# A fused attention and expert kernel: the first expert blocks loaded inside the last attention group

## The chip, the cores and the metric

The kernel runs on one core of a Trainium2 chip. TensorE (PE in the profile) multiplies, VectorE (DVE) and ScalarE (ACT) do elementwise work, GpSimd (POOL) and SyncE (SP) issue DMAs, POOL those that scatter rows by an index. The metric is the device time of one execution in microseconds (us), as the median of several.

## The reference, cut to what matters

There are 8 batches of 2,496 rows. The attention output becomes the expert layer's input, row by row; each token has one expert of eight, given by a hash of its id.

```python
scores = (1.0 / S) * np.matmul(z, z.transpose(0, 2, 1))   # z: (8, 2496, 64)
attn = np.maximum(scores, 0.0) ** 2
x = (u * np.matmul(attn, v)).reshape(B * S, D)             # D = 256
expert_idx = token_ids * np.int64(2654435761) % np.int64(E)   # E = 8
for e in range(E):
    mask = expert_idx == e
    out[mask] = np.maximum(x[mask] @ w1[e], 0.0) @ w2[e]   # w1: 256x1024, w2: 1024x256
```

With the inputs used, the experts have 2,506, 2,446, 2,582, 2,478, 2,498, 2,473, 2,434 and 2,551 tokens.

## The kernel before, in words

The tile framework derives every wait from what an instruction reads and writes; the order of instructions on each engine is the order in which the program issues them (`order = tc.manual_schedule()`, line 439). An instruction that waits holds back all that stands behind it on its engine or queue.

**Attention.** A batch's rows make 20 tiles, 19 of 128 rows and one of 64. Four tiles make a group, so there are 5 groups a batch and 40 in all (line 453), written here as (batch, group), the last (7,4). For each group the loop of lines 475 to 523 runs over the inner tiles t: `attend` (line 253) accumulates attention times v in PSUM, `square` and `turn_scores` prepare squared scores, and `scores` of the next group stand near the group's end. Scores are symmetric: in batches after the first, a block that is already made for one group is turned by DVE into a "mirror" tile (`turn_scores`, line 207) and read from there by a later group. There are six mirror tiles of 128 x 2048 numbers, in a pool that opens with group 4 and closes behind the last group (`mirror_pool`, lines 472, 482 and 527). `attend_short` (line 226) does the short tile of a batch, `gate` and `gate_short` multiply with u and give rows of x on DVE.

**Routing.** `places` (line 297) is a generator whose small steps, one per call of `between` (line 457), are strewn over the first groups: from the token ids it counts tokens by expert (matmuls at line 345, copies at 346, a scan at 350), and works out each token's slot. Slots are ordered by expert, each expert padded to blocks of 256 slots, at most 85 blocks. Steps with a bare `yield` (line 336) are idle. `enter` then writes the token numbers by slot to memory, and the list comes back as `idx` (line 428): the token of each slot, or N for an empty slot. `eb_i` holds each block's expert, `used` the number of blocks in use. `place_x` (line 430) scatters a tile of x rows to their slots in `x_rows` (`x_dram` in the code) by a POOL DMA; it too is called from `between`.

**Experts.** After the last group all remaining `place_x` calls are issued. For each block of 256 slots, `load_w` (line 541) reads the block's expert number into a register on SP and issues five DMAs for the two weight matrices, `load_x` (line 550) issues four for the block's x, `turn_x` (line 558) transposes it on DVE, `up` (line 562) is the first layer with its relu on ACT or DVE, `down` (line 576) the second layer for 128 slots, with a copy on ACT and a scatter to the output by a POOL DMA (rows with an index beyond the output are skipped). `run` (line 588) strings blocks together: `up` of block j runs between the two `down` of block j - 1, and loads run two blocks ahead into three sets of buffers. The weights' buffers are a pool of their own, which lies where the mirror tiles were.

**Tail.** 79 blocks run unconditionally, then a branch on `used` (line 615) covers blocks 81 to 84, which are made if more than 81 are in use, and the last two blocks follow behind it. On an untaken branch each engine jumps over its part and brings the semaphore counts up to date.

Of the kernel before, what the change touches and what calls it, by code (L numbers as in the profile page):

```python
# [10 lines left out]
F32 = mybir.dt.float32  # L11
BF16 = mybir.dt.bfloat16
I32 = mybir.dt.int32
AF = mybir.ActivationFunctionType
OP = mybir.AluOpType
AX = mybir.AxisListType
# [8 lines left out]
def kernel(  # L25
# [10 lines left out]
    nc = tc.nc  # L36

    B, S, D = u.shape
    K = z.shape[-1]
    N = B * S  # L40
    E, _, F = moe_w1.shape
# [3 lines left out]
    P = 128  # L45
    TM = S // P
    SM = TM * P
    R = S - SM
    T = TM + 1
    assert R == 64 and K == 64  # L50
    G = 4
    NG = T // G
# [12 lines left out]
    def pool(name, bufs, **kw):  # L65
        return ctx.enter_context(tc.tile_pool(name=name, bufs=bufs, **kw))
# [81 lines left out]
    def turn_z(b, g):  # L148
        if g == 0:
            zT[b] = zpool.tile([P, T * P], F32, name="zT")  # L150
        o = zT[b][:, ts(g, G * P)]
        if b:
            nc.vector.transpose(o, zn[b][:, ts(g, G)].rearrange("p t j k -> p (t j k)"))
            return
        ps = mm_ps.tile([P, G * P], F32, name="z_ps", tag="mm")
        for i, t in enumerate(group(g)):
            nc.tensor.transpose(ps[:, ts(i, P)], zn[b][:, t].rearrange("p h k -> p (h k)"), ident[:])  # L157
        nc.scalar.copy(o, ps[:])
# [76 lines left out]
    def gate_short(b, ps):  # L235
        nc.scalar.copy(odd[:], ps[R:P, :])  # L236
        x = x_sb[b, NG - 1] = xpool.tile([P, G, D], F32, name="x_sb")
        nc.vector.tensor_add(odd[:], odd[:], ps[0:R, :])  # L238
        nc.vector.scalar_tensor_tensor(out=x[0:R, G - 1, :], in0=odd[:], scalar=c2, in1=u_sb[b, NG - 1][0:R, G - 1, :],
                                       op0=OP.mult, op1=OP.mult)  # L240
        gated.append((b * T + TM, x[0:R, G - 1, :]))
# [11 lines left out]
    def attend(b, g, t, acc, queries):  # L253
        for i in queries:
            if i in whole(g):
                nc.tensor.matmul(acc[i // 2][:, i % 2, :], lhs(b, g, t, i), v_sb[b][:, t, :],  # L256
                                 start=(t == 0 and i % 2 == 0), stop=(t == TM - 1), skip_group_check=True)
# [15 lines left out]
    idx = const.tile([P, NS], I32)  # L273
    eb_i = const.tile([1, NB], I32)
    used = const.tile([1, 1], I32)
    slot_i = const.tile([P, C], I32)
    addr = const.tile([P, C], I32)
    token = const.tile([P, B, T], I32)
# [18 lines left out]
    def places():  # L297

        with tc.tile_pool(name="route", bufs=1) as route:
# [33 lines left out]

            for _ in range(6):
                yield
            total = route.tile([P, E, C], F32)
            rank = route.tile([P, E, C], F32)
            H = 512 // C  # L340
# [40 lines left out]
            nc.vector.tensor_sub(shift[:], ends[:], blocks[:])  # L381
            yield
            nc.vector.scalar_tensor_tensor(shift[:], shift[:], float(BLK), first[:], op0=OP.mult, op1=OP.subtract)
            yield


# [68 lines left out]
    i = 0  # L455
# [13 lines left out]
            place_x()  # L469
        i += 1  # L470

    mirror_pool = ExitStack()
    scores(0, 0)
    square(EARLY)
    for n, (b, g) in enumerate(groups):
        if n + 1 < len(groups):
            load_u(*groups[n + 1])
        if g == 0 and b + 1 < B:
            load_z(b + 1)
            load_v(b + 1)  # L480
        if n == NG - 1:
            m = mirror_pool.enter_context(tc.tile_pool(name="mirror", bufs=1))
            mirrors = [m.tile([P, G, G, P], F32, name=f"m_{k}") for k in range(NG * NG // 4)]

        acc = [acc_ps.tile([P, 2, D], F32, name="acc", tag="acc") for _ in range(2)]
        for k in range(2):
            for t in range(EARLY):
                attend(b, g, t, acc, [2 * k, 2 * k + 1])
            square(2)
            turn_scores(2)  # L490
            between()
        for t in range(EARLY, TM - LATE):
            if g == NG - 1 and b + 1 < B and t % 2 == 0 and t // 2 <= NG:
                turn_z(b + 1, t // 2 - 1)
            attend(b, g, t, acc, range(G))
            if t % G == G - 1 and (b, t // G, g) in mirror and g < NG - 1:
                mirrors.append(mirror.pop((b, t // G, g)))
            square(2)
            turn_scores(2 + (t % 3 == 0))
            between()  # L500
        assert not to_square
        if g == NG - 1:
            gate_short(b, attend_short(b))
            mirrors.extend(mirror.pop(k) for k in sorted(mirror))
        attend_last(b, g, acc)
        between()
        if n + 1 < len(groups):

            while len({k[:3] for k in to_turn}) + len(fresh(*groups[n + 1])) // G > NG + (g + 1 < NG):
                turn_scores(1)  # L510
            scores(*groups[n + 1])
        square(3)
        turn_scores(3)

        for k in range(2):
            for t in range(TM - LATE, TM):
                attend(b, g, t, acc, [2 * k, 2 * k + 1])
            for q in (2 * k, 2 * k + 1):
                gate(b, g, q, acc)
            square(2)  # L520
            turn_scores(2)
            between()
        between()
    assert not to_turn and next(place, None) is None and i > 2 * T + 4 * C
    while gated:
        place_x()
    mirror_pool.close()

    LOADS = 3
    wpool = pool("wpool", 1)
    opool = pool("opool", 4)
    w1_buf = [wpool.tile([P, DP, F], F32, name=f"w1_{k}") for k in range(LOADS)]
    w2_buf = [wpool.tile([P, FP, D], F32, name=f"w2_{k}") for k in range(LOADS)]
    xg_all, xT_all = (zpool.tile([P, T * P], F32, name="zT") for _ in range(2))
    xg_buf = [xg_all[:, ts(k, DP * BLK)].rearrange("p (k d) -> p k d", d=D // NQ) for k in range(LOADS)]
    xT_buf = [xT_all[:, ts(k, DP * BLK)].rearrange("p (k h i) -> p k h i", h=DP, i=Q) for k in range(LOADS)]
    w1, w2, xg, xT, hT = {}, {}, {}, {}, {}

    def load_w(j, k):
        w1[j], w2[j] = w1_buf[k], w2_buf[k]
        e = nc.sync.value_load(eb_i[0:1, j:j + 1], min_val=0, max_val=E - 1)
        for r in range(NQ):
            rows = moe_w1[ds(e, 1), ts(r, D // NQ)].rearrange("one d f -> (one d) f")
            nc.sync.dma_start(w1[j][ts(r, Q)], rows.rearrange("(h i) f -> i h f", i=Q))
        nc.sync.dma_start(
            w2[j][:], moe_w2[ds(e, 1)].rearrange("one f d -> (one f) d").rearrange("(c p) d -> p c d", p=P))

    def load_x(j, k):  # L550

        xg[j] = xg_buf[k]
        for r in range(NQ):
            nc.sync.dma_start(
                xg[j][ts(r, Q)],
                x_dram[ts(j, BLK), ts(r, D // NQ)].rearrange("(k i) d -> i k d", i=Q))

    def turn_x(j, k):
        xT[j] = xT_buf[k]
        nc.vector.transpose(xT[j].rearrange("p k h i -> p (k h i)"), xg[j].rearrange("p k d -> p (k d)"))  # L560

    def up(j, f):
        ps = mm_ps.tile([P, 2, BLK], F32, name="h_ps", tag="mm")
# [9 lines left out]
        else:  # L573
            nc.vector.tensor_scalar_max(o, ps[:], 0.0)  # L574

    def down(j, t):
        ps = acc_ps.tile([P, D], F32, name="o_ps", tag="acc")
        for f in range(FP):
            nc.tensor.matmul(ps[:], hT[j][:, f, ts(t, P)], w2[j][:, f, :], start=(f == 0), stop=(f == FP - 1))  # L579
        o = opool.tile([P, D], F32, name="o_sb")  # L580
        nc.scalar.copy(o[:], ps[:])  # L581
        st = nc.gpsimd.indirect_dma_start(  # L582
            out=out[:], out_offset=bass.IndirectOffsetOnAxis(ap=idx[:, j * TB + t:j * TB + t + 1], axis=0),
            in_=o[:], in_offset=None, bounds_check=N - 1, oob_is_err=False)
        tc.declare_no_dep(st.ins, group="rows", reason="each token has its own row")
        tc.add_to_no_dep_group("rows", st.ins)

    def run(first, last, loads):

        for j in range(first, last + 1):  # L590
            if j < last and j + 2 < loads:
                load_x(j + 2, (j + 2) % LOADS)
            for f in range(0, FP, 2):
                if j < last:
                    up(j, f)
                if j > first and f % 4 == 2:
                    down(j - 1, f // 4)
                if f == 2 and j < last and j + 1 < max(last, loads):
                    turn_x(j + 1, (j + 1) % LOADS)
            if j < last and j + 2 < loads:  # L600
                load_w(j + 2, (j + 2) % LOADS)
# [3 lines left out]

    NU = -(-N // BLK) + E // 2 - 1
    NM = NU - 2
    for j in range(2):
        load_w(j, j)
    for j in range(2):  # L610
        load_x(j, j)
    turn_x(0, 0)
    run(0, NM, NU)
    n_used = nc.values_load(used[0:1, 0:1], min_val=1, max_val=NB)
    with tc.If(n_used > NU):
        for j in range(NU, NB):
            load_x(j, (NM + 2) % LOADS)
            load_w(j, (NM + 2) % LOADS)
            turn_x(j, (NM + 2) % LOADS)
            run(j, j + 1, 0)  # L620
    run(NM, NU, 0)

    order.__exit__(None, None, None)
# [28 lines left out]
```

## Time and profile before

| | us |
|---|---|
| median of 3 runs | 2717.02 (2716.9 to 2718.02) |
| profiled execution, its own time | 2718.32 |
| its span in the profile | 2716.4 |
| PE busy | 2681.2 (99%) |
| DVE busy | 1190.3 (44%) |
| ACT busy | 576.2 (21%) |
| POOL busy | 478.7 (18%) |
| expert matmuls, both layers (L566, L579) | 587.2 + 585.2 |

Times in the trace count from the span's start. PE is the matmul row, PEld its weight loads, which overlap. Matmuls on 32-bit numbers appear as two records each. "L566" is line 566 of the kernel before. A bracket at a line's end tells how long the engine stood idle before it and what released it. Names of DMA queues end in q (SPq, POOLq). Buffers that share a pool's tag appear by the tag's name: x of a block and its transpose are both zT, the weights w. Attention ends and the expert layer begins at about 1572 us; the branch of the tail lies at about 2681 us.

### The profile page before, as it was taken

Reading aid. Unit: us, or ns where it says so; the run is one execution under the profiler, and the core shown is the slowest. Engines: PE = TensorE matmul, PEld = TensorE weight load, DVE = VectorE, ACT = ScalarE, POOL = GpSimd, SP = SyncE. Lnnn points to the kernel's source line nnn. Section 1 sums busy time; section 2 is a strip of 40 time slices with the busy share of each in tenths; the row PEclk is TensorE's granted clock in tenths of the full one; section 3 lists DMA queues with packets and bytes.
Section 4 is the critical chain, followed back from the end, with each engine's and each line's share of the span. In section 5 each row is a group of like instructions: output and inputs, shape, how many; then the busy total and the mean of one; then the engine's idle time right before and its main releaser. Section 6 shows DMA issues by size and latency. Waiting matters only on the chain.

```text
span 2716.4 us, 32950 instructions
## 1 busy us (share of the span) xinstructions
PE 2681.2 (99%) x12650; PEld 2250.2 (83%) x12650; DVE 1190.3 (44%) x1875; ACT 576.2 (21%) x1151; POOL 478.7 (18%) x500
## 2 busy tenths in 40 slices
PE   8999999999999999999999979999999999999998
PEld 6777887888888887887878868888888888888887
DVE  5655956848838838758659411111111111111111
ACT  2013214214222233123132101111111111111111
POOL 0221222122212221222101111111111111111111
PEclk9999999999999999999999989999999999999999
DMA  9612113013103121031101077777777777777773
GB/s 283 212 31 73 32 31 88 16 32 88 31 23 82 31 50 60 26 89 32 32 15 31 23 191 189 188 188 188 194 190 193 191 189 191 190 189 188 189 186 104
DMA packets 334256, 308.84 MB, mean 114 GB/s; under 512 B 186732, under 2 KB 293117, under 8 KB 334096
## 3 DMA queue, kind: packets, MB, share of 16 engines
q1 hardware_dynamic: 309424, 264.78, 38.5%
q0 software_dynamic: 20496, 41.10, 5.0%
q8 instruction: 102, 1.67, 0.3%
q10 hardware_dynamic: 4176, 0.82, 0.2%
q14 instruction: 58, 0.48, 0.1%
HBM read 243.25 MB, written 64.13 MB: 113 GB/s over the span
## 4 chain that ended last, share of the span: by engine, by line
PE 55%; issue 37%; POOL 6%; DMA 2%; POOLq 0%; DVE 0%
PE acc L256 44%; PE s_ps L181 8%; POOL out_dram L582 5%; PE acc L250 1%; DMA out_dram<-o_sb,idx 1%; PE q_ps L231 1%; DMA zn<-in_z_dram 0%; POOLq L582 0%; POOL x_rows L433 0%; PE z_ps L157 0%; DVE upto L350 0%; DVE x_sb L265 0%; DVE a L202 0%; POOLq L647 0%; PE cnt_ps L345 0%
## 5 line engine op out<-in xcount | busy, mean ns | idle before, releaser
L256 PE MATMUL acc<-v_sb,a 128*128 128x256 f32 x3760 | 826.8, 380 | 2.5 <-DVE a L202 1.4
L256 PEld LDWEIGHTS acc<-v_sb,a 128*128 128x128 f32 x3760 | 711.0, 190 | 128.0 <-issue 29.0
L215 DVE STREAM_TRANSPOSE m<-a 32x512 f32<-32x512 f32 (+1 forms) x1120 | 757.2, 676 | 19.5 <-ACT a L200 2.7
L566 PE MATMUL h_ps<-zT,w 128*128 128x256 f32 x2592 | 587.2, 380 | 16.5 <-DMA zT<-x_rows 15.3
L579 PE MATMUL o_ps<-w,hT 128*128 128x256 f32 x2592 | 585.2, 379 | 0.0
L566 PEld LDWEIGHTS h_ps<-zT,w 128*128 128x128 f32 x2592 | 493.6, 191 | 84.6 <-issue 15.7
L579 PEld LDWEIGHTS o_ps<-w,hT 128*128 128x128 f32 x2592 | 492.5, 190 | 66.9
L574 DVE TENSOR_SCALAR hT<-h_ps 128x512 f32<-128x512 f32 x162 | 112.0, 691 | 951.4 <-PE h_ps L566 951.4
L256 PE MATMUL acc<-v_sb,m 128*128 128x256 f32 x2016 | 439.7, 379 | 0.0
L256 PEld LDWEIGHTS acc<-v_sb,m 128*128 128x128 f32 x2016 | 383.1, 190 | 52.0
L188 ACT ACTIVATE a<-s_ps 128x512 f32<-128x512 f32 (+1 forms) x365 | 193.6, 593 | 913.5 <-PE s_ps L181 905.0
L433 POOL DMA_INDIRECT x_rows<-x_sb,slot_i x160 | 157.8, 986 | 1089.8 <-DVE x_sb L265 917.1
L582 POOL DMA_INDIRECT out_dram<-o_sb,idx x162 | 157.5, 972 | 978.8 <-ACT o_sb L581 964.0
L181 PE MATMUL s_ps<-zT 64*128 64x512 f32 (+1 forms) x1040 | 230.4, 586 | 0.0
L186 DVE TENSOR_SCALAR a<-s_ps 128x512 f32<-128x512 f32 (+1 forms) x155 | 106.0, 684 | 283.1 <-PE s_ps L181 282.0
L200 ACT ACTIVATE a<-a 128x512 f32<-128x512 f32 (+1 forms) x420 | 221.5, 623 | 0.0
L581 ACT COPY o_sb<-o_ps 128x256 f32<-128x256 f32 x162 | 60.3, 372 | 743.7 <-PE o_ps L579 743.7
L181 PEld LDWEIGHTS s_ps<-zT 64*128 64x128 f32 x1040 | 116.8, 187 | 89.1 <-issue 61.5
L421 POOL DMA_INDIRECT slot_tokens<-token,addr x160 | 159.3, 996 | 161.2 <-DVE addr L415 110.9
L572 ACT ACTIVATE hT<-h_ps 128x512 f32<-128x512 f32 x162 | 96.7, 597 | 242.1 <-PE h_ps L566 242.1
L265 DVE SCALAR_TENSOR_TENSOR x_sb<-acc,u_sb 128x256 f32<-128x256 f32 x152 | 57.7, 419 | 58.4 <-PE acc L256 57.8
L238 DVE TENSOR_TENSOR odd<-odd,q_ps 64x256 f32<-64x256 f32 x8 | 3.3, 414 | 168.9 <-ACT odd L236 168.9
(67 smaller groups left out, 331.5 us busy)
## 6 DMA issues: line engine op xcount, KB each, us to landing
w<-in_moe_w_dram SPq DMA_DIRECT2D x324, 256.0 KB, 6.7
w<-in_moe_w_dram SPq DMA_DIRECT2D x81, 1024.0 KB, 6.1
x_rows<-zero SPq DMA_DIRECT2D x10, 2176.0 KB, 15.0
zT<-x_rows SPq DMA_DIRECT2D x324, 64.0 KB, 6.0
v_sb<-in_v_dram SPq DMA_DIRECT2D x32, 512.0 KB, 4.5
u_sb<-in_u_dram SPq DMA_DIRECT2D x32, 512.0 KB, 4.0
zn<-in_z_dram SPq DMA_DIRECT2D x28, 304.0 KB, 5.6
v_sb<-in_v_dram SPq DMA_DIRECT2D x8, 384.0 KB, 7.3
```

The costliest lines, as they stand in the source:

```text
L181: nc.tensor.matmul(ps[:, 0:n], zT[b][h, ts(t, P)], zT[b][h, ds(g * G * P, n)], start=True, stop=True)
L186: nc.vector.tensor_scalar_max(a, ps[:, 0:n], 0.0)
L188: nc.scalar.activation(a, ps[:, 0:n], AF.Relu)
L200: nc.scalar.square(o, x)
L215: nc.vector.transpose(mirror[b, a, g][ts(c, Q)].rearrange(squares)[:, 0:m, ts(r, Q)], made[b, a, g][ts(r, Q)].rearrange("p t (s q) -> p (t ...
L256: nc.tensor.matmul(acc[i // 2][:, i % 2, :], lhs(b, g, t, i), v_sb[b][:, t, :], start=(t == 0 and i % 2 == 0), stop=(t == TM - 1), skip_gr ...
L421: st = nc.gpsimd.indirect_dma_start(out=slot_dram[:, None], out_offset=bass.IndirectOffsetOnAxis(ap=addr[0:n, c:c + 1], axis=0), in_=token ...
L433: st = nc.gpsimd.indirect_dma_start(out=x_dram[:, :], out_offset=bass.IndirectOffsetOnAxis(ap=slot_i[0:width(c % T), c:c + 1], axis=0), in ...
L566: nc.tensor.matmul(ps[:, i, :], w1[j][:, c, ts(f + i, P)], xT[j][:, :, c, :], start=(c == 0), stop=(c == DP - 1))
L574: nc.vector.tensor_scalar_max(o, ps[:], 0.0)
L579: nc.tensor.matmul(ps[:], hT[j][:, f, ts(t, P)], w2[j][:, f, :], start=(f == 0), stop=(f == FP - 1))
L582: st = nc.gpsimd.indirect_dma_start(out=out[:], out_offset=bass.IndirectOffsetOnAxis(ap=idx[:, j * TB + t:j * TB + t + 1], axis=0), in_=o[ ...
```

## The change

In the last group, (7,4), and without a branch, the program now issues: the weights of block 0 at inner tile 5, the x of blocks 0 and 1 at inner tile 10, the turns of both at inner tiles 14 and 15, and the weights of block 1 after the short tile. The weights' buffers are the six mirror tiles themselves: the two that are free in the last group for block 0, the four that it reads for blocks 1 and 2. The pool of mirrors no longer closes, and the weights' own pool is gone.

At inner tile 10 the rows of group (7,4) are not yet in `x_rows`. Tokens are numbered so that late tokens have the last places within their expert; `places` works out, per expert, the slot of the first late token (`late`), the least of these (`least`), and whether it lies within the first two blocks: `redo` is N (19,968) then and 0 otherwise, `good` is N if it does not and 0 otherwise. These are five new steps of `places`, and five of the six idle ones are gone. `extra` is `used` plus `redo` and takes its place in the branch. If the branch is taken, it now also makes blocks 0 and 1 again, besides 81 to 84.

The output scatters of the branch move behind it: its results go to `o_all`, a tile of 128 x 5120 numbers that POOL clears before block 0, and twelve scatters from there follow the branch on POOL in any case. Two small DVE maxima make `once` and `again`, the index lists of blocks 0 and 1 for their first and second making; of the two, only the first writes rows when `redo` is 0. POOL takes no part in the branch any more; PE, ACT, DVE and SP do.

```diff
@@ places
-            for _ in range(6):
-                yield
+            yield
...
+            late = route.tile([P, E], F32)
+            nc.vector.tensor_add(late[:], shift[:], upto[:, :, C - G - 1])
+            yield
+            least = route.tile([P, 1], F32)
+            nc.vector.tensor_reduce(least[:], late[:], axis=AX.X, op=OP.min)
+            yield
+            for o, op in ((redo, OP.is_lt), (good, OP.is_ge)):
+                nc.vector.tensor_scalar(o[:], least[:], float(AHEAD * BLK), float(N), op0=op, op1=OP.mult)
+                yield
+            nc.vector.tensor_add(extra[:], used[:], redo[0:1, :])
+            yield
@@ the loop over groups
-            m = mirror_pool.enter_context(tc.tile_pool(name="mirror", bufs=1))
+            m = pool("mirror", 1)
...
+            if n + 1 == len(groups) and t == T // 4:
+                w_buf = list(mirrors)
+                w_buf.extend(mirror[b, a, g] for a in range(NG - 1))
+                load_w(0, 0)
+            if n + 1 == len(groups) and t == T // 2:
+                assert not gated
+                xg_all, xT_all = (zpool.tile([P, T * P], F32, name="zT") for _ in range(2))
...
+                for k in range(AHEAD):
+                    load_x(k, k)
+            if n + 1 == len(groups) and t >= TM - LATE - AHEAD:
+                turn_x(t - (TM - LATE - AHEAD), t - (TM - LATE - AHEAD))
...
             gate_short(b, attend_short(b))
+            if n + 1 == len(groups):
+                load_w(1, 1)
@@ before the expert blocks
-    wpool = pool("wpool", 1)
+    o_all = vpool.tile([P, T, D], F32, name="v_sb")
+    nc.gpsimd.memset(o_all[:], 0.0)
+
+    once = const.tile([P, AHEAD * TB], I32)
+    again = const.tile([P, AHEAD * TB], I32)
+    for o, x in ((once, redo), (again, good)):
+        nc.vector.tensor_tensor(o[:], idx[:, 0:AHEAD * TB], x[:].to_broadcast([P, AHEAD * TB]), op=OP.max)
@@ down
-        o = opool.tile([P, D], F32, name="o_sb")
+        k = j * TB + t
+        if later is not None:
+            o = o_all[:, len(later), :]
+            later.append((o, again[:, k:k + 1] if j < AHEAD else idx[:, k:k + 1]))
+        else:
+            o = opool.tile([P, D], F32, name="o_sb")
         nc.scalar.copy(o[:], ps[:])
+        if later is None:
+            store(o[:], once[:, k:k + 1] if j < AHEAD else idx[:, k:k + 1])
@@ the tail
-    for j in range(2):
-        load_w(j, j)
-    for j in range(2):
-        load_x(j, j)
-    turn_x(0, 0)
     run(0, NM, NU)
-    n_used = nc.values_load(used[0:1, 0:1], min_val=1, max_val=NB)
+    n_used = nc.values_load(extra[0:1, 0:1], min_val=1, max_val=NB + N, engines=[
+        mybir.EngineType.PE, mybir.EngineType.Activation, mybir.EngineType.DVE, mybir.EngineType.SP])
+    later = []
     with tc.If(n_used > NU):
-        for j in range(NU, NB):
+        for j in [*range(AHEAD), *range(NU, NB)]:
             load_x(j, (NM + 2) % LOADS)
             load_w(j, (NM + 2) % LOADS)
             turn_x(j, (NM + 2) % LOADS)
-            run(j, j + 1, 0)
+            run(j, j + 1, 0, later)
+    for o, rows in later:
+        store(o, rows)
     run(NM, NU, 0)
```

## The prediction

> **What bounds the kernel now.** I began with the page. TensorE (PE) is busy 99% of the span, so a time can change only where PE stands still, runs at a lower clock, or gets other work. PE's work is the same matmuls before and after. The second part of the page, 40 slices of 67.9 us, shows one hole, the "7" in the 24th slice (1562 to 1630 us), and the granted clock lower in the same slice. The group of the first expert layer names its cause: x, 15.3 us.
>
> ```profile
> PE   8999999999999999999999979999999999999998
> PEclk9999999999999999999999989999999999999999
> ...
> L566 PE MATMUL h_ps<-zT,w 128*128 128x256 f32 x2592 | 587.2, 380 | 16.5 <-DMA zT<-x_rows 15.3
> ```
>
> Next the list of waits, where PE's own lines are few; the third is in the first batch:
>
> ```profile
> PE h_ps L566 <- DMA zT<-x_rows: 15.3, 1, 15.3
> ...
> PE h_ps L566 <- ACTq L615: 1.2, 1, 1.2
> ...
> PE acc L256 <- DVE x_sb L265: 1.1, 1, 1.1
> ```
>
> Then the timeline at 1563 to 1588 us. The last attention matmul (L256, from 1571.65, 0.38 us) ends at 1572.03. The last rows of x leave POOL at 1574.04, SP can ask for x only when they have landed, at 1581.61, DVE turns block 0 at 1586.52, and PE starts at 1587.33. The weights of blocks 0 and 1 (4 MB) go out only from 1566.18, after the last reader of the mirror tiles, and share the DMA engines with those last rows.
>
> ```profile
> 1566.18 1.93 SPq L546 DMA_DIRECT2D w<-in_moe_w_dram  x4
> ...
> 1574.04 0.97 POOL L433 DMA_INDIRECT x_rows<-x_sb,slot_i  x1 [0.31 <-issue]
> 1581.61 5.76 SPq L554 DMA_DIRECT2D zT<-x_rows  x12
> 1586.52 0.71 DVE L560 STREAM_TRANSPOSE zT<-zT 128x512 f32<-128x512 f32 x1 [14.02 <-DMA zT<-x_rows]
> ...
> 1587.33 12.36 PE L566 MATMUL h_ps<-zT,w 128*128 128x256 f32 x48 [15.30 <-DMA zT<-x_rows]
> ```
>
> Last the same place by windows (columns: window, its us, busy of PE, PEld, DVE, ACT, POOL, then granted clock, DMA share, GB/s). After the hole PE runs at half clock until about 1591.
>
> ```profile
> 1572.00:1587.30 15.30, 0.03 (x1) 0.00 (x0) 1.14 (x2) 0.00 (x0) 2.40 (x3) 0.67 1.02 273
> 1587.30:1589.10 1.80, 1.77 (x4) 1.51 (x5) 0.00 (x0) 0.00 (x0) 0.00 (x0) 0.50 0.40 92
> 1589.10:1591.00 1.90, 1.90 (x6) 1.47 (x5) 0.00 (x0) 0.00 (x0) 0.00 (x0) 0.53 0.86 235
> 1591.00:1593.00 2.00, 2.00 (x11) 1.77 (x10) 0.18 (x1) 0.60 (x1) 0.00 (x0) 1.00 1.01 207
> ```
>
> **Change, 1: block 0 is ready before attention ends.** Weights 0 go to two mirror tiles last read in group (7,3) at inner tiles 4 to 11, about 1509.5 to 1526.8; SP has been idle since 1507.8 (it stood 57.0 us in front of the weight loads, by its own waits). Five DMAs issue in 2.5 us and land in 6.7: in place by about 1536. The eight x DMAs wait for the four scatters of group (7,3), the last of which issues at 1543.72; with a landing of 2.4 us (8.4 at most in this stretch) they issue from 1547.1 (1553) for 8 x 0.48 = 3.8 us and land 6.0 us later: 1557 (1563). DVE turns two blocks, 2 x 0.7 us, done by 1558.5 (1564.5). Behind these turns on DVE stands the short tile's add at 1567.37, and behind the x loads on POOL the short tile's scatter at 1568.51: both later than the later value. So PE can go on at 1572.03: **-15.30 us**.
>
> **2: the clock.** 48 matmul records after the hole take 12.36 us; 48 in the tail take 10.52 (2670.06). Without the hole that is **-1.84 us** (half clock over 3.9 us would say 1.95; I take the records). Here a rule is to be weighed: the tail's 1.2 us stall leaves the clock at 1.00, the 15.3 us hole does not. The Trainium skill (TensorE: Matmul & The Clock Gate, Part 1: The HAM clock gate) puts the limit at an idle window of about 3.4 us. By the rows alone, any remaining stall over 1.2 us might keep the 1.84 us; by the rule only one over 3.4. For the main sum both say the same, as no stall remains; for the rivals I use the rule.
>
> **3: blocks 1 and 2 in time?** Block 0 has no second-layer work of a predecessor, so it lasts 32 records, 6.9 us: block 1 is due at 1578.9, block 2 (13.8 later) at 1592.8. Weights 1 wait for the first two mirrors of group (7,4) to be read by the short pass (L231 from 1562.36, 0.46 us per four matmuls): issue about 1563.5 to 1566.3, landed 1573: 6 us early. Block 2's x waits for the last scatter (1574.04, landing 2.4 to 8.4 us): 1576.4 to 1582.4, plus 2 us of issue and 6 us: 1584.5 to 1590.5. Its first-layer weights issue behind it on SP: 2.5 us and 6.7 us more: landed 1588 to 1594. Taken: 1588, since only 2 MB instead of 4 compete with the scatters. Cost 0; at the far end 1.2 us. DVE waits for this x with only a relu behind it that is due at 1589. From block 3 on the SP order is the old one.
>
> **4: the new steps on POOL and DVE before block 0.** POOL clears a 128x5120 tile: the 128x1280 memset took 1.16 us, so an estimated 4.6 us, from 1575.0 to 1579.6, ahead of the first result store at about 1588. The Trainium skill (SBUF — State Buffer, SBUF: two separate sides) speaks against it: GpSimd and some VectorE forms share a port pair by exclusive lock. No run here shows the two together. By the trace the two small maxima (128x4, nearest row 0.16 us) cost 0.3 us of DVE; by the rule they might wait 4.6 us. The first relu behind them is needed at 1582.4 (first second-layer matmul), so by either the sum is 0; without that cover it is at most 4.6.
>
> **5: the routing steps five slots earlier.** Five idle slots go, five small DVE operations (0.15 us each, DVE has gaps there) come later, so the number of slots stays. The count matmuls move to after 7 inner tiles instead of 12: 24.17 + 56 records x 0.2187 = 36.4 us, and the mask they need is done at 32.58. DVE's two last pairs of squares now wait for counts, until 38.9 and 40.9; PE needs the first of them at 52.9 (the short tile, L250). Scan and rank sums (5.8 us) run in the gap at 46.8 to 52.8, before the next relu at 55.45. What it gives: in group 1 the 2.82 us scan stood between two gates and made PE wait.
>
> ```profile
> 67.80 2.82 DVE L350 TENSOR_TENSOR_SCAN upto<-ones,total 128x1280 f32<-128x1280 f32 x1
> 70.53 0.73 DVE L265 SCALAR_TENSOR_TENSOR x_sb<-acc,u_sb 128x256 f32<-128x256 f32 x2
> ...
> 71.32 26.17 PE L256 MATMUL acc<-v_sb,a 128*128 128x256 f32 x120 [1.11 <-DVE x_sb L265]
> ```
>
> The scan's place is taken by a 0.16 us operation: **-1.11 us**.
>
> **6: the tail.** Expert 0 has 2,506 tokens in slots 0 to 2,505, and the late 448 tokens of 19,968 are some 50 of them, so the first late slot is near 2,455, not below 512: the branch stays untaken and blocks 0 and 1 stand. PE's stall of 1.2 us there follows ACT's count at 2681.7, behind its copy, and stays (0). PE's own branch took 3.94 us on its sequencer (2677.2 to 2681.2, the branch line's rows), mostly behind queued matmuls; it now jumps over six block bodies instead of four. One row can't tell whether that matters: taken 0, and if it grew with the bodies, to 5.9 us, PE would start 1.9 later. New are twelve stores on POOL between branch and last two blocks, every row out of range. The trace has one such store: expert 2 has 2,582 tokens, so tile 1 of its last block is empty, the 62nd store:
>
> ```profile
> 2025.18 0.97 POOL L582 DMA_INDIRECT out_dram<-o_sb,idx  x1 [5.93 <-ACT o_sb L581]
> ...
> 2681.31 0.97 POOL L582 DMA_INDIRECT out_dram<-o_sb,idx  x1 [2.48 <-ACT o_sb L581]
> 2696.59 0.97 POOL L582 DMA_INDIRECT out_dram<-o_sb,idx  x1 [14.31 <-ACT o_sb L581]
> ...
> 2710.36 0.97 POOL L582 DMA_INDIRECT out_dram<-o_sb,idx  x1 [2.48 <-ACT o_sb L581]
> ```
>
> It costs no more than the others. Back to back POOL takes 1.28 us a scatter (1572.76 to 1574.04): 12 x 1.28 = 15.4 us, from 2682.6 to 2698.0 in the old times. The store due at 2696.59 is 1.4 us late, the next (2703.50) on time, the end not moved. They become path once each takes more than (2710.36 - 3 x 1.28 - 2682.6)/12 = 2.0 us.
>
> **Sum.** 15.30 + 1.84 + 1.11 = 18.25. Profiled span 2716.40 - 18.25 = 2698.15; the profiled run's own 2718.32 gives 2700.07; it was 1.30 above the median of the runs, 2717.02, which gives **2698.8**.
>
> **Rivals.** (B) *Block 1 or 2 starves.* For it: DMA is at its share of 1.0 around the hole. Against: half the bytes compete. A stall of 1 to 4 us, with the clock's 1.84 above 3.4: 2700 to 2704.6. (C) *The tail turns slower.* The twelve stores serialise on their landings: 12 x 5.4 us (the median of these stores) = 64.8, from 2682.6 to 2747.4; the last store then goes at 2751.2 instead of 2710.36, 40.9 later: 2739.7. It decides from 2.0 us a store, and eats the gain at 3.5. Against: the wait of a store is for the one eight before it, 10 us back. (D) *The early loads do not come early*, because the x loads wait for the last scatters after all: only step 5 and part of the weights' crowding are won, about 2712 to 2716. Against: the scatters of the last group come later in the program than the loads.
>
> **How the numbers follow.** A 0.80 (own range 2697.3 to 2700.7, with the jump's 1.9), B 0.11, D 0.04, C 0.05. A change within 0.2%, 5.4 us, can hardly be told from none here; and D lies there. Faster 0.91, same 0.04, slower 0.05. For 8 in 10 the range takes A and B: 2697.0 to 2704.0.
>
> **What would show it.** PE's wait for zT gone from the waits, clock 1.00 at 1570 to 1592, x loads issued near 1547, no PE wait on x_sb near 71, twelve stores 1.28 us apart with no longer last gap. Wrong, if PE waits for weights or x in blocks 1 or 2, or if the last store comes late behind the twelve.

## The result, and the profile after

| | before | after |
|---|---|---|
| median of the runs, us | 2717.52 (4 runs, 2716.9 to 2718.03) | 2699.97 (4 runs, 2699.02 to 2701.16) |
| profiled execution, its own time | 2718.32 | 2699.9 |
| span | 2716.4 | 2698.2 |

The ratio of the runs is 0.9933, with a 95% interval of 0.9921 to 0.9945: 17.6 us faster, against 18.25 forecast; the range held. The span, 2698.2, was forecast as 2698.15.

The second part of the page of the changed kernel, and the group of the first expert layer (its line is now L600): the hole and the dip of the clock are gone, and of that group's 16.5 us of waiting 1.2 are left.

```profile
PE   8999999999999999999999999999999999999998
PEclk9999999999999999999999999999999999999999
...
L600 PE MATMUL h_ps<-zT,m 128*128 128x256 f32 x2592 | 585.3, 379 | 1.2 <-ACTq L655 1.2
```

All of PE's waits that its list has are these; x_sb in the first batch is gone too, and what is left was there before:

```profile
PE z_ps L157 <- DMA zn<-in_z_dram: 9.2, 1, 9.2
...
PE acc L256 <- DVE a L202: 1.4, 1, 1.4
PE h_ps L600 <- ACTq L655: 1.2, 1, 1.2
```

The timeline at the seam. SP asks for x of blocks 0 and 1 at 1544.57, 25 us before PE needs it; DVE turns both by 1552.2; PE's last attention group runs into the first expert matmuls with nothing between (1566.00 + 4.15 = 1570.15; ends of matmuls are modelled and overlap a little). Block 2's x and weights follow at 1574.57 and 1577.21.

```profile
1544.57 3.79 SPq L496 DMA_DIRECT2D zT<-x_rows  x8
1548.37 0.71 DVE L512 STREAM_TRANSPOSE zT<-zT 128x512 f32<-128x512 f32 x1 [7.75 <-DMA zT<-x_rows]
1551.48 0.71 DVE L512 STREAM_TRANSPOSE zT<-zT 128x512 f32<-128x512 f32 x1 [2.41 <-DMA zT<-x_rows]
...
1561.60 1.87 SPq L506 DMA_DIRECT2D m<-in_moe_w_dram  x4
...
1566.00 4.15 PE L256 MATMUL acc<-v_sb,a 128*128 128x256 f32 x18
1569.99 10.52 PE L600 MATMUL h_ps<-zT,m 128*128 128x256 f32 x48
...
1573.17 4.37 POOL L589 MEMSET v_sb<- 128x5120 f32 x1
1573.64 0.69 DVE L608 TENSOR_SCALAR hT<-h_ps 128x512 f32<-128x512 f32 x1 [2.88 <-PE h_ps L600]
1574.57 1.79 SPq L496 DMA_DIRECT2D zT<-x_rows  x4
```

And the tail, with the first and the last of the twelve new stores (of v_sb), and the first and the last of the four stores that follow them:

```profile
2662.62 10.63 PE L600 MATMUL h_ps<-zT,m 128*128 128x256 f32 x48 [1.22 <-ACTq L655]
2663.41 0.98 POOL L625 DMA_INDIRECT out_dram<-v_sb,again  x1 [0.30 <-issue]
...
2677.49 0.98 POOL L625 DMA_INDIRECT out_dram<-v_sb,idx  x1 [0.30 <-issue]
...
2678.78 0.98 POOL L625 DMA_INDIRECT out_dram<-o_sb,idx  x1 [0.30 <-issue]
...
2691.19 0.97 POOL L625 DMA_INDIRECT out_dram<-o_sb,idx  x1 [2.48 <-ACT o_sb L620]
```

**Where the 18.2 us of the span went.** The wait for the first z, and four distances between marks, in both traces:

| stretch | before | after | difference |
|---|---|---|---|
| start to the first matmul (wait for z) | 9.46 | 9.15 | -0.31 |
| first matmul to the end of attention | 1562.57 | 1561.00 | -1.57 |
| end of attention to the first second-layer matmul | 1572.03 to 1599.53: 27.50 | 1570.15 to 1580.35: 10.20 | -17.30 |
| that matmul to the start of the last store | 1110.83 | 1110.84 | 0.0 |
| start of the last store to the end | 6.05 | 7.01 | +0.96 |

The sum is -18.2. The first difference is chance (the z wait of other runs lies between 9.2 and 9.5 us); the next three are the steps of the prediction; the last is a cost that it did not have.

### The profile page after: what moved, and what is told of

Read it like the earlier page. It is cut to its first block, busy times and chain, and to the rows that moved or that the text cites. A ratio compares the mean times of both kernels' runs of the same rounds, so it can differ in the third digit from the quotient of the medians.

```text
span 2698.2 us, 32995 instructions
## 1 busy us (share of the span) xinstructions
PE 2678.7 (99%) x12650; PEld 2248.9 (83%) x12650; DVE 1191.3 (44%) x1882; ACT 576.4 (21%) x1151; POOL 495.8 (18%) x513
## 5 line engine op out<-in xcount | busy, mean ns | idle before, releaser
L600 PE MATMUL h_ps<-zT,m 128*128 128x256 f32 x2592 | 585.3, 379 | 1.2 <-ACTq L655 1.2
L613 PE MATMUL o_ps<-m,hT 128*128 128x256 f32 x2592 | 585.2, 379 | 0.0
L600 PEld LDWEIGHTS h_ps<-zT,m 128*128 128x128 f32 x2592 | 492.4, 190 | 68.5 <-ACTq L655 1.6
L613 PEld LDWEIGHTS o_ps<-m,hT 128*128 128x128 f32 x2592 | 492.5, 190 | 67.0
L181 PE MATMUL s_ps<-zT 64*128 64x512 f32 (+1 forms) x1040 | 230.4, 586 | 0.0
L181 PEld LDWEIGHTS s_ps<-zT 64*128 64x128 f32 x1040 | 116.9, 187 | 89.1 <-issue 61.5
```

Of the source, the lines that this page charges most:

```text
L181: nc.tensor.matmul(ps[:, 0:n], zT[b][h, ts(t, P)], zT[b][h, ds(g * G * P, n)], start=True, stop=True)
L600: nc.tensor.matmul(ps[:, i, :], w1[j][:, c, ts(f + i, P)], xT[j][:, :, c, :], start=(c == 0), stop=(c == DP - 1))
```

## The experiments

All times are medians; "changed" is the changed kernel, 2699.97, or 2699.79 (5 runs) where it ran again on the chip of the experiment, as here:

> The changed kernel once more, to stand beside the next three on one chip: 2700.0, and from the last packet of the last store to the end of POOL's drain 3.9 us, against 2.9 in the kernel before.

Measured: 2699.79 (2699.35 to 2700.74), ratio 0.9932 (0.9919 to 0.9946). In its trace the last packet of the last store ends 4.98 us ahead of the span's end, where the kernel before has 4.03 (both to the span's end, where the expectation counts to the drain's, so each is some 1.1 above the expectation's figures): the 0.96 us shows again.

### The x loads late, the weights early

```diff
-                for k in range(AHEAD):
-                    load_x(k, k)
-            if n + 1 == len(groups) and t >= TM - LATE - AHEAD:
-                turn_x(t - (TM - LATE - AHEAD), t - (TM - LATE - AHEAD))
...
     while gated:
         place_x()
+    for k in range(AHEAD):
+        load_x(k, k)
+    for k in range(AHEAD):
+        turn_x(k, k)
```

> The changed kernel, with only the x loads and turns of blocks 0 and 1 put back behind the last scatters; the weights of block 0 stay early. Theory (the hole is the chain scatter, landing, x load, turn): the scatters now share the DMA engines with 2 MB of weights instead of 4, so the last lands some 2.4 us after its issue instead of 7.6; x issues near 1574.6 and takes 5.7 us to the turn and PE as before, so PE waits some 10 us (1570.1 to 1580.3) and loses 1.84 to the clock: 2700.0 + 12 = 2712. Rival (the weights were the hole, by filling the DMA engines): PE waits under 3 us and the time is under 2704.

Measured: 2712.13 (2710.91 to 2713.47), ratio to before 0.998 (0.997 to 0.999). The timeline of this kernel: SP can ask 2.46 us after the last scatter's issue, not 7.57 as before, and PE waits 8.9 us, not 15.3.

```profile
1571.93 0.97 POOL L449 DMA_INDIRECT x_rows<-x_sb,slot_i  x1 [0.30 <-issue]
...
1574.39 5.74 SPq L496 DMA_DIRECT2D zT<-x_rows  x12
1578.06 0.71 DVE L512 STREAM_TRANSPOSE zT<-zT 128x512 f32<-128x512 f32 x1 [7.67 <-DMA zT<-x_rows]
1578.83 12.86 PE L600 MATMUL h_ps<-zT,m 128*128 128x256 f32 x48 [8.90 <-DVE zT L512]
```

So the hole of before had two layers. 8.9 us of it are the chain scatter, landing, load, turn, which only an earlier load of x removes. The other 6.4 us came from the weights: in the kernel before, the 4 MB of both blocks, issued from 1566.18, were under way together with the last scatter and made it land late, and x behind it; here block 0's went out long before. The next experiment, which sends both late again, confirms it: there too the next x load goes out 7.59 us after the last scatter (1572.34 to 1579.93). The rival, that the weights were the whole hole, is out.

### The weights of block 0 late, x early

The swap of the buffers makes block 0's weights wait for the short pass, as they do in the kernel before.

```diff
                 w_buf.extend(mirror[b, a, g] for a in range(NG - 1))
-                load_w(0, 0)
...
             if n + 1 == len(groups):
+                w_buf = w_buf[2:4] + w_buf[0:2] + w_buf[4:]
+                load_w(0, 0)
                 load_w(1, 1)
```

> The changed kernel, with only the weights of block 0 put back to after the short tile, in front of those of block 1 (4 MB in one go from about 1561.6); x stays early. Theory: block 0's first-layer weights issue in 2 us and land in 6.7, at about 1570, as PE arrives at 1570.1: PE waits 0 to 1.5 us, the clock stays full, the last scatters land late again but block 2 is due only at 1590.7: 2700.0 to 2701.5. Rival (early weights are worth as much as early x): a stall over 3.4 us with the clock's loss, 2705 or more.

Measured: 2700.85 (2700.29 to 2701.69), ratio 0.9938 (0.9921 to 0.9954): 0.9 slower than the changed kernel, which is within the spread of the runs. Block 0 starts without a wait at 1570.17; block 1 has the only one at the seam, and the clock stays full.

```profile
1578.09 3.69 PE L601 MATMUL h_ps<-zT,m 128*128 128x256 f32 x16 [0.84 <-DVE hT L609]
```

The relu named there, over at 1577.97, isn't what it waited for: the profile names the last event before it, and in the changed kernel PE runs on into block 1 without a pause though that relu starts only at 1577.09. Block 1's weights, sent last, are the cause: in the trace, the semaphore that the first weight load of this matmul waits for gets the last count of its DMA at 1577.95. With x early, the early weights of block 0 are worth only these 0.84 us. The two parts of the change don't add up: early weights alone save 6.4 us of wait, early x alone nearly everything.

### Holes of known size before the first expert matmul

```diff
-                turn_x(t - (TM - LATE - AHEAD), t - (TM - LATE - AHEAD))
+                if t == TM - LATE - 1:
+                    turn_x(1, 1)
...
     while gated:
         place_x()
+    for _ in range(3):
+        turn_x(0, 0)
```

The same with two and with eleven turns; the result of the extra turns is that of the first.

> The changed kernel, with the turn of block 0 put behind the last gates on DVE and made three times: a hole of known size before the first expert matmul. Three turns of 0.65 to 0.71 us from 1570.6: PE starts near 1572.7, a hole of 2.5 us. By the page's window of about 3.4 us the clock stays at 1.00 and the time is 2700.0 + 2.5 = 2702.5. If any stall over 1.2 us cost the clock: 2704.3.

> As the hole of three turns, with eleven: PE starts near 1577.9, a hole of 7.7 us, which holds a whole idle window wherever the windows lie. Theory (hole and clock are two terms): half clock for some 3.5 to 4 us after the hole, 2700.0 + 7.7 + 1.8 = 2709.5. If the 1.84 us after the hole had another cause (weights or x of the first block arriving late), nothing is lost after the hole here: 2707.7.

> As the hole of three turns, with two: a hole of about 1.9 us. The hole of 2.63 us brought half clock, the stalls of 0.84 and 1.2 us did not. If what counts is the share of one 3.41 us window that PE stands still, and more than half is needed, 1.9 us can do it only if it lies within one window: 2702.1 with the clock kept, 2703.8 with it lost; the granted clock says which. Rival (an idle window of 3.4 us is needed, and the hole of 2.63 us was a chance): clock kept.

| turns | PE waits | from the end of attention to the first second-layer matmul, less 10.20 | lost beside the wait | time | over the changed kernel |
|---|---|---|---|---|---|
| 2 | 1.88 | 1570.00 to 1584.04: 3.84 | 1.96 | 2704.92 (2704.28 to 2705.51) | 4.95 |
| 3 | 2.63 | 1569.39 to 1584.17: 4.58 | 1.95 | 2704.82 (2704.46 to 2705.54) | 4.85 |
| 11 | 8.60 | 1570.65 to 1592.52: 11.67 | 3.07 | 2712.57 (2711.05 to 2713.11) | 12.60 |

The ratios to the kernel before are 0.9951 (0.9935 to 0.9966), 0.9954 (0.9937 to 0.9971) and 0.9979 (0.997 to 0.9989). That wait and clock are two terms is shown: with the weights and x long there, 2 to 3 us are lost beside the wait. But my expectation for three turns, that the clock would stay up because 2.6 us is less than an idle window, was wrong, and so was the rule as I had read it from the Trainium skill (TensorE: Matmul & The Clock Gate, Part 1: The HAM clock gate): even 1.88 us cost 3.41 us of half clock.

Wherever half clock begins and ends within a trace here, it lasts 3.41 us or two to five times that, so the clock seems to be set in steps of 3.41 us; they begin at another time in each trace. These are the steps around the cut, first of the kernel with two turns, then of the kernel before (columns as in the prediction: PE's busy time stands behind the comma, the granted clock is the third number from the end):

```profile
1569.88:1573.29 3.41, 1.53 (x8) 1.25 (x7) 1.87 (x5) 0.00 (x0) 2.76 (x4) 1.00 0.51 169
1573.30:1576.71 3.41, 3.41 (x10) 2.66 (x9) 0.00 (x0) 0.60 (x1) 3.41 (x1) 0.50 0.31 85
1576.72:1580.13 3.41, 3.41 (x17) 3.02 (x16) 0.69 (x1) 0.60 (x1) 0.67 (x1) 1.00 0.69 174
```

```profile
1570.42:1573.83 3.41, 1.61 (x8) 1.08 (x6) 1.18 (x3) 0.00 (x0) 1.95 (x2) 1.00 1.03 250
1573.84:1577.25 3.41, 0.00 (x0) 0.00 (x0) 0.00 (x0) 0.00 (x0) 0.97 (x1) 1.00 1.07 304
1577.26:1590.90 13.64, 3.57 (x9) 2.88 (x10) 0.71 (x1) 0.00 (x0) 0.00 (x0) 0.50 0.89 233
```

With two turns PE is at work again from 1571.89, and the clock falls only at 1573.30, at the end of a step in which PE stood for 1.88 us. In the kernel before, PE stood for 1.80 us of the step in which the hole begins, and the next step still had the full clock. With three turns all 2.63 us lay in one step, and the clock fell at its end, 1572.04. The stalls of 0.84 us (weights of block 0 late) and of 1.1 to 1.5 us (tail) never did it. So on these traces, one for each kernel, what counts is how long PE stands still within one step, and the limit lies between 1.8 and 1.9 us. A stall of 2 or 3 us that is cut in two by the edge of a step might then cost nothing beside its length; no trace here has one.

With eleven turns half clock lasted for 5.71 us of PE's work, in the kernel before for 3.57, with two and three turns for 3.41. Half of that is lost, and 0.16 us more, as the first expert matmul no longer starts ahead of the modelled end of the last attention one (1569.99 against 1570.15 in the changed kernel): 3.02, 1.95 and 1.87 us, where 3.07, 2.00 and 1.95 to 1.96 were measured.

Most of the rest in the last column is in the tail, which is not part of the edit: PE stands there for 0.3 us (three and eleven turns) or 1.35 us (two turns) more, between matmuls, for nothing that the profile shows, as here with two turns. It stands so for 0.4 us with the weights of block 0 late too; with eleven turns some 0.6 us remain without a place.

```profile
2683.59 0.38 PE L603 MATMUL h_ps<-zT,m 128*128 128x256 f32 x1 [1.02 <-issue]
```

1.88 + 1.96 + 1.35 = 5.2 and 2.63 + 1.95 + 0.33 = 4.9 us: that is why two and three turns cost the same. What stalls PE there stays open; the instruction stream after the branch is a guess that no run here tests.

### The routing steps alone

The kernel before, with this only:

```diff
-            for _ in range(6):
-                yield
+            yield
             total = route.tile([P, E, C], F32)
...
             nc.vector.scalar_tensor_tensor(shift[:], shift[:], float(BLK), first[:], op0=OP.mult, op1=OP.subtract)
             yield
+            for _ in range(5):
+                yield
```

> The kernel before, with five of the six idle routing slots moved behind the shift step: the count matmuls five slots earlier, nothing else. Theory: the 1.11 us wait of PE on x_sb near 71 us is gone, and the last count no longer stands alone between the short tile and the scores (0.4 us): attention ends 1.1 to 1.6 us earlier, 2717.5 - 1.4 = 2716.1. Rival (DVE's squares come late and PE waits for them in group 0): 0 or slower. The hole before the experts stays at 15.3 us.

Measured: 2716.81 (2716.08 to 2717.31) against 2718.45 for the kernel before on this chip; ratio 0.9994, interval 0.9985 to 1.0004, so the times alone can't tell it from nothing. The trace can: PE's wait on x_sb is not among its waits, those on x for block 0 and at the branch are (15.0 and 1.2 us), and from the first scores (L181 at 13.04) to the end of attention it takes 1556.44 us, where the kernel before takes 1558.14 from 13.89. That is 1.7 us; in the changed kernel it was 1.57. The part over 1.11 fits the last count matmul, which no longer stands alone between the short tile and the scores; it was not measured by itself. The rival, squares that come late, is out.

### The twelve stores: inside the branch, and twice

```diff
-    n_used = nc.values_load(extra[0:1, 0:1], min_val=1, max_val=NB + N, engines=[
-        mybir.EngineType.PE, mybir.EngineType.Activation, mybir.EngineType.DVE, mybir.EngineType.SP])
+    n_used = nc.values_load(extra[0:1, 0:1], min_val=1, max_val=NB + N)
...
         if later is None:
             store(o[:], once[:, k:k + 1] if j < AHEAD else idx[:, k:k + 1])
+        else:
+            store(*later[-1])
...
-    for o, rows in later:
-        store(o, rows)
```

> The changed kernel, with the twelve stores inside the branch and POOL taking part in the branch again, as before. Theory (POOL's last drain grows with the stores since POOL last settled its store semaphores, which the untaken branch does): the drain is back at 2.9 us past the last packet, 2699.0. Rival (the drain's 0.98 us is chance or has to do with the kernel's other stores): 2700.0. If the twelve stores had cost PE or the last stores anything, the last store would also come earlier than 19.17 us ahead of the kernel before; I expect it does not.

> The kernel with the stores inside the branch once more, to stand beside the early read on one chip: 2699.2, against the changed kernel's 2700.0.

```diff
-    for o, rows in later:
-        store(o, rows)
+    for _ in range(2):
+        for o, rows in later:
+            store(o, rows)
```

> The changed kernel, with the twelve stores behind the branch made twice. Theory (1.28 us a store on POOL, hidden up to 27 us): 24 x 1.28 = 30.7 us from 2663.4 to 2694.1, then the four last stores back to back, the last at 2697.9 instead of 2691.19: 6.7 us later, and the drain a further 1 us if it grows with the number of stores: 2706.7 to 2707.7. Rival (stores with no row in range cost POOL less back to back, or the queue takes more than eight): the last store moves under 2 us. Rival (they serialise on landing): over 25 us later.

| stores behind the branch | time | PE's start after the branch to the last store | last packet of a store to the span's end |
|---|---|---|---|
| none, kernel before | 2718.45 | 2681.79 to 2710.36: 28.57 | 4.03 |
| none, stores in the branch | 2699.18 and 2698.55 (trace of the first) | 2661.84 to 2690.42: 28.58 | 4.02 |
| 12, changed | 2699.79 | 2662.77 to 2691.35: 28.58 | 4.98 |
| 24 | 2707.57 | 2662.04 to 2697.33: 35.29 | 5.96 |

The ratios to before are 0.9931 (0.9917 to 0.9944) and 0.9928 (0.9914 to 0.9941) for the stores in the branch, and 0.9961 (0.9946 to 0.9976) for 24 stores. Both expectations hold, that of the stores in the branch by the trace: 0.6 us of time is within the spread of the runs. Twelve stores hide entirely behind the last two blocks; the second twelve push the last store back by 6.72 us (6.7 expected), so a store with no row in range costs POOL its full 1.28 us back to back, and neither rival is right. And the drain of POOL at the end grows by 0.95 to 0.98 us per twelve stores, some 80 ns a store. The drains themselves, in the changed kernel and in the one with the stores in the branch (number, then shortest, median and longest in ns):

```profile
L689 POOLq DRAIN  x3: 40/108/6435, 2691.0 to 2697.9; - x3
```

```profile
L688 POOLq DRAIN  x3: 40/113/5455, 2690.2 to 2696.2; - x3
```

With POOL in the branch, the untaken path brings POOL's store semaphores up to date, at a time when POOL has nothing to do (the rows of the branch's line):

```profile
L656 POOLq INC_SWDGE_SEM  x1: 1127/1127/1127, 2664.4 to 2664.4; - x1
```

That this is the reason is argued; that the 0.96 us belongs to stores behind the branch is shown. So the version with the stores in the branch is the better one, by 0.96 us in the trace.

### The branch's number read early

```diff
+    n_used = nc.values_load(extra[0:1, 0:1], min_val=1, max_val=NB + N)
     run(0, NM, NU)
-    n_used = nc.values_load(extra[0:1, 0:1], min_val=1, max_val=NB + N)
```

> As the kernel with the stores inside the branch, and the number that the branch tests is read into each engine's register before the expert blocks instead of at the branch. ACT's 0.48 us read no longer lies between its last copy and the branch, so its count comes 0.5 us earlier; PE's own branch (over at 0.6 us past its last matmul) is then the later one: the stall of 1.2 us becomes 0.7 to 0.8, the time 2698.7 against 2699.2. Rival (PE's branch sets the stall already): no difference.

Measured: 2698.91 (2698.32 to 2699.71), ratio 0.9929 (0.9915 to 0.9943), against 2698.55 without it: no gain, as the rival has it. ACT was indeed early, but PE's own branch took 4.7 us in this trace, ended later, and PE's stall stayed at 1.2 us.

```profile
L656 PEldq COMPARE_BRANCH  x1: 4715/4715/4715, 2658.1 to 2658.1; - x1
L656 ACTq COMPARE_BRANCH  x1: 54/54/54, 2662.3 to 2662.3; - x1
```

PE's untaken branch took 3.94 us before, and 3.91 to 4.72 in the traces that jump over six bodies: it did not grow to the 5.9 us that the prediction's upper end had in proportion to the bodies.

### The branch taken

```diff
-            nc.vector.tensor_add(extra[:], used[:], redo[0:1, :])
+            nc.vector.tensor_add(extra[:], used[:], good[0:1, :])
```

> The changed kernel, with the branch made to be taken (N added to the number of blocks where the early blocks stand, in place of where they don't): what an input pays whose late tokens reach into the first two blocks. Six blocks one after the other, each with 0.5 us to read its expert, 2.5 us to issue and 6.7 us to land its weights, 6.9 and 6.9 us of matmuls with nothing between, some 1 us of copies and waits, and half clock for some 3.5 us after each wait for weights: 24.5 + 1.8 = 26 us each, 157 in all, 2857. Rival (a block's weights come while the block before still multiplies, as w1's buffer is free after its first layer): 6 us less each, 2820.

Measured: 2792.77 (2791.45 to 2793.97), ratio 1.0271 (1.0254 to 1.0289): 92.8 us over the untaken branch. Both figures were too high. The first block waits 6.2 us for weights; then the blocks follow each other in 14.4 us (matmuls of the first layer from 2699.56, 2714.03, 2728.39), since the next block's first-layer weights are issued as the second layer starts (2692.17 and 2691.98, say) and most of their loading fits under its 7 us. The rival was right in this, but not in its sum. An input whose late tokens lie in the first two blocks would lose some 74 us by this change, not win 17.6.

## Why the prediction was right

**Step 1, block 0 ready.** Right: -15.30, and with the clock -17.30 measured. x was turned earlier than reckoned (by 1552.2, against 1556.6 with the shift of 1.9 us): its first loads landed in less than 4 us, not in 6.

**Step 2, the clock.** Mechanism and size were right: from the first expert matmul to the first of the second layer the kernel before takes 12.20 us and the changed one 10.36, 1.84 less; the 2.00 by the distance from attention's end holds the 0.16 us of overlap besides. The side figure, half clock over 3.9 us, was misread: it lasted for 3.57 us of PE's work. As a number the term is no constant: the runs show 1.95 to 3.07. The rule weighed there, that a stall up to 3.4 us is free, fell. The main sum didn't use it, but rival B did, and would have been priced too low at the small end: a stall of 2 us can cost 4.

**Step 3, blocks 1 and 2.** Right, and to within 0.2 us once the shift of 1.9 us is taken off: weights 1 issued at 1561.60, block 2's x at 1574.57.

**Step 4, POOL and DVE.** Right. The clearing took 4.37 us (4.6 estimated), the maxima 0.15 and 0.16, ahead of the clearing. The port rule was misread: by the Trainium skill (SBUF — State Buffer, SBUF: two separate sides) a VectorE operation with two SBUF inputs is held only against a GpSimd operation that reads SBUF, and the clearing only writes. No run has maxima and clearing at the same time. Operations with one input did meet it: the relus at 1573.64 and 1577.09 (from PSUM, the second in the clearing in part) took 0.69 us as ever, and in the run with eleven turns of x (from SBUF) five of them lie within the clearing and took 0.71 us each, as those outside, and the clearing 4.36.

**Step 5, routing.** Right in place; the term was 1.57 to 1.7, not 1.11.

**Step 6, the tail.** The branch stayed untaken, and the stores behaved as worked out (1.28 us each, the first of the last four 1.4 us late, the last not at all). Its "the end not moved" failed by 0.96 us: the cost lies after the last store, in POOL's drain, where I had not looked. It is cancelled by three surpluses, 0.46 us in step 5, 0.16 beside the clock and the 0.31 of the wait for z: the span's agreement to 0.1 us is luck. The median came out 1.2 us above the forecast because I took the profiled run's distance of 1.3 us to the median of three runs as lasting; the profiled execution's own time, 2699.9, was forecast as 2700.07.

**The rivals.** B and D didn't come true; what they need was made in two experiments (weights late, x late), and the prices were near: a stall of 0.84 us for B's 1 to 4, and 2712.13 for D's 2712 to 2716. C is out by the stores' spacing.

## What to carry to other kernels

A hole between two phases is a chain, and what else shares the DMA engines sets how long its links are: take out the link that can't be hidden (here the load that waits for the last scatter) before the bytes that stretch it. Price a stall of TensorE by the clock as well as by its length: here 2 us of standing still, all in one step of the clock, cost 4. And work that is moved to an idle queue can still be paid for at its end: look at the last drain, not only at the last instruction.

## What was not expected of the hardware

The clock was cut after stalls of 1.88 and 2.63 us, once 1.4 us after PE had resumed work, and then for 3.41 us. POOL's last drain grew by some 80 ns for each indirect store behind the branch, although with twelve of them the last packet was over at 2678.33, 12.9 us ahead of the last store. A store whose rows are all out of range still sends 48 packets, with 576 bytes in all in place of some 131,000, and takes POOL as long as a full one.
